# Transposing attention rows with the DMA crossbar, and a by-class layout for the dilated half

## The chip, the cores and the metric

The kernel runs on one NeuronCore of a Trainium2 chip. The metric is the device time of one execution in microseconds. The core's engines each run their own instruction stream in order: TensorE (PE; its weight loads are shown as PEld), VectorE (DVE), ScalarE (ACT), GpSimd (POOL) and SyncE (SP). SP and POOL also issue DMAs, which run on 16 DMA engines that all queues share.

## The reference

Eight heads of causal attention in eight batch rows are followed by an MLP over all tokens. Heads 0 to 3 see a sliding window of 32 positions; heads 4 to 7 see every fourth position of the last 128 (dilation 4).

```python
batch, n_heads, seq, head_dim = (8, 8, 576, 64)
rel = pos[:, None] - pos[None, :]
mask_plain = (rel >= 0) & (rel < window)                      # window = 32
mask_dil = (rel >= 0) & (rel < window * dilation) & (rel % dilation == 0)
...
attn = np.exp(scores); attn = attn / (np.sum(attn, axis=-1, keepdims=True) + 1e-09)
attn_out = np.matmul(attn, v)
x = attn_out.transpose(0, 2, 1, 3).reshape(B * S, H * D)      # 4608 x 512
h = x @ w_in                                                  # 512 x 2048
r = np.maximum(h, 0.0)
out = (r * r) @ w_out                                         # 2048 x 512
```

## The kernel before

**Two streams of work.** The program is written as a hand-interleaved order. Attention goes by batch row b, 576 tokens each. The MLP goes by chunk c of 512 tokens, nine in all. The loop at L786 takes rows 2 to 7: its iteration b runs the attention of row b, and between the attention's steps `pump(n)` issues n steps of the MLP of chunk b-1 (`moe_gen`), so that TensorE always has matmuls to do. A step is about two matmuls of 512 columns (first product, `mm1_gen`) or four of 256 columns (second product, by a Strassen-like scheme with seven block products, `mm2_strassen_gen`); a chunk has 60 steps in all, 32 of them in the first product. From row 4 on, 8 steps go ahead of the attention, 3 stand at each gap, and what is left follows at the end (`pump(1000)`). Row 3 has 16 ahead, row 2 has 24 and other gaps. Chunks 7 and 8 follow after the loop, with no attention beside them.

**A row's attention.** `attn_scores` makes the scores (`s_sliding`, L557; `s_dilated`, L576), the exponential on ACT (L547) and the mask product on DVE (L548). `attn_values` then makes the value products: three sliding ones (`av_sliding`, L605, tiles `pav`) and four dilated ones (`av_dilated`, L619, tiles `paw`), each followed by `normalize` on DVE (a reciprocal, L590, and a product, L591), which writes a tile x with tokens on partitions. All score and value tiles in PSUM come from one pool of two buffers (`papool`, tag "pa"), used in turn. Four transposing steps, `x_sliding` (L634, tiles `px`, 6 transposes each) and `x_dilated` (L652, tiles `py`, 8 each), turn x on TensorE so that features lie on partitions, and a copy on ACT (L640, L658) puts it into `xT`, a ring over four rows, in token order. `mm1_half` (L294) reads `xT` as the moving operand. As 512 is less than 576, chunk b needs most of row b as its last part.

**DVE's share of the MLP.** Each of the 16 blocks of the first product goes through a relu on ACT (L317) and a square on DVE (L318). Three larger DVE steps serve the Strassen scheme: sums of g (L327, L328), one difference in g when the second product begins (L402), and one later (L414). They stand in DVE's order where the chunk's steps put them.

**Fetching the next row.** While row b is worked on, row b+1 is fetched: `after_transposes` puts a one-element copy `seen` on POOL that waits until row b's q and k transposes have landed; behind it POOL issues the loads of the sliding q and k (`ns`, L111) and the dilated ones (`dd`, L202, into DRAM). At hook 3, after the last scores, `turn` runs: DVE regroups `ns` by token (`nr`, L119), and SP issues, in this order, its store to DRAM (`dp`, L212), the loads of v (`sv`, `sd`) and the crossbar transposes from DRAM that make `QKTp` (L220) and `QKTd` (L224), two each. All transposes stand in SP's queue.

**Stores.** A finished chunk goes out from SP, per half of 256 tokens, in rows of 2 KB (`leave`, L393); chunks 0 and 1 are stored by 128 tokens (`store`, L452). The last chunk goes out in column halves.

**Dilated classes.** The 144 positions of a class (token index modulo 4) are worked on in two blocks of 72 queries. `QD`, `PADD` and `OWND` hold these sizes.

Of the kernel before, what the change touches and what calls it, by code (L numbers as in the profile page):

```python
# [8 lines left out]
FP16 = mybir.dt.float16  # L9
# [4 lines left out]
P = 128  # L14
# [3 lines left out]
def kernel(  # L18
# [30 lines left out]
    CL = S // DIL  # L49
    QD = CL // 2  # L50
    PADD = (48, P - QD)
    OWND = (CL - 64, 64)
    KPAD = 64
# [5 lines left out]
    natp = ctx.enter_context(tc.tile_pool(name="natp", bufs=2))  # L59
    xp = ctx.enter_context(tc.tile_pool(name="xp", bufs=4))  # L60
    gp = ctx.enter_context(tc.tile_pool(name="gp", bufs=2))
# [10 lines left out]
    XW = 4 * S  # L72
    xT = const.tile([P, NDM, XW], FP16, name="xT")
    wi_cols = (512, 512, 1024)
# [58 lines left out]
    def load_dilated_v(b, eng):  # L133
        vv = v[b, HH:H].rearrange("h (i c) d -> i h (c d)", c=DIL)
        i0 = 0
        for t in range(2):
            eng.dma_start(out=sd[P - OWND[t] : P, t, :, :], in_=vv[i0 : i0 + OWND[t]])
            i0 += OWND[t]

# [115 lines left out]
    hi_ = const.tile([P, QB], FP16, name="hi_")  # L255
    md = maskd.rearrange("p (n t w) -> p n t w", t=2, w=QD)
    for m, w, pad in (
        (maskp.rearrange("p (n w) -> p n w", w=QB), QB, PADP),
        (md[:, :, 0], QD, PADD[0]),
        (md[:, :, 1], QD, PADD[1]),  # L260
    ):
        nc.vector.tensor_scalar(
            out=lo_[:, 0:w], in0=relf[:, 0:w], scalar1=-pad - 0.5, scalar2=None, op0=ALU.is_gt
        )
        nc.vector.tensor_scalar(
            out=hi_[:, 0:w], in0=relf[:, 0:w], scalar1=W - pad - 0.5, scalar2=None, op0=ALU.is_lt
        )
        nc.vector.tensor_mul(
            m,
            lo_[:, 0:w].unsqueeze(1).to_broadcast([P, m.shape[1], w]),  # L270
            hi_[:, 0:w].unsqueeze(1).to_broadcast([P, m.shape[1], w]),
        )
# [15 lines left out]
    def mm1_half(c, ffc, ph, dmks):  # L288
        lo = c * TOKC % XW
        cut = min(TOKC, XW - lo)  # L290
        parts = [(0, cut, lo)] + ([(cut, TOKC, 0)] if cut < TOKC else [])
        for dmk in dmks:
            for t0, t1, x0 in parts:
                nc.tensor.matmul(  # L294
                    ph[:, t0:t1],
                    wi4[ffc // 4][:, dmk, :, ffc % 4],
                    xT[:, dmk, x0 : x0 + t1 - t0],
                    start=(dmk == 0 and t0 == 0),
                    stop=(dmk == NDM - 1),
                    skip_group_check=len(parts) > 1,  # L300
                )
# [45 lines left out]
    w_sums = sums_of_w_out()  # L347

    def mm2_strassen_gen(c, g):
        A, Bk, Ck = "abc"  # L350
# [39 lines left out]
        def leave(o, i, js):  # L390
            t0 = c * TOKC + HTOK * i
            m = slice(HM * js[0], HM * (js[-1] + 1))
            nc.sync.dma_start(  # L393
                out=out[t0 : t0 + HTOK, m].rearrange("(t p) m -> p t m", p=P), in_=o[:, :, m]
            )

# [50 lines left out]
    def store(c, t, po):  # L447
        if t % 2 == 0:
            halves[c] = otp.tile([P, 2, DM], FP32, name=f"ot{c}_{t}", tag="ot")
        ot = halves[c][:, t % 2]  # L450
        nc.scalar.copy(ot, po)
        (nc.sync if c else nc.gpsimd).dma_start(out=out[(c * 4 + t) * P : (c * 4 + t + 1) * P, :], in_=ot)  # L452

# [113 lines left out]
    def s_dilated(b, g):  # L567
        tiles = [pa(f"pz{b}_{g}_{h}") for h in range(2)]
        for h, ps in enumerate(tiles):
            for a in range(2):  # L570
                for t in range(2):
                    q0 = KPAD + (2 * g + h) * CL + QD * t
                    for e in range(2):
                        r = slice(D * e, D * (e + 1))
                        n = 2 * a + t
                        nc.tensor.matmul(  # L576
                            ps[:, e, QD * n : QD * (n + 1)],
                            QKTd[b % 2][r, 1, a, q0 - PADD[t] : q0 - PADD[t] + P],
                            QKTd[b % 2][r, 0, a, q0 : q0 + QD],
                            start=True,  # L580
                            stop=True,
                        )
        for h, ps in enumerate(tiles):
            softmax(4 + 2 * g + h, ps, maskd)

    def normalize(b, what, pav, w):
        x = xp.tile([QB, 2, HH, D], FP16, name=f"x{b}_{what}", tag="x")
        rcp = xp.tile([QB, 2, HH], FP32, name=f"rcp{b}_{what}", tag="rcp")
        pv = pav[0:w, :, 0 : HH * (D + 2)].rearrange("p i (h d) -> p i h d", d=D + 2)
        nc.vector.reciprocal(rcp[0:w], pv[:, :, :, D])  # L590
        nc.vector.tensor_tensor(  # L591
            out=x[0:w],
            in0=pv[:, :, :, 0:D],
            in1=rcp[0:w].unsqueeze(3).to_broadcast([w, 2, HH, D]),
            op=ALU.mult,
        )
        return x

    def av_sliding(b, mp):
        pav = pa(f"pav{b}_{mp}")  # L600
        for i in range(2):
            m = 2 * mp + i
            for h in range(HH):
# [7 lines left out]
                )  # L611
        return normalize(b, f"p{mp}", pav, QB)

    def av_dilated(b, t, a):
        pav = pa(f"paw{b}_{t}_{a}")
        for e in range(2):
            for h in range(HH):
                off = e * 288 + a * 144 + t * QD
                nc.tensor.matmul(  # L619
# [5 lines left out]
                )  # L625
        return normalize(b, f"d{t}_{a}", pav, QD)

    def x_sliding(b, half, xs, wide):
        px = pt(f"px{b}_{half}", wide)
        for m3 in range(3):  # L630
            m = 3 * half + m3
            x = xs[m // 2][:, m % 2].rearrange("p h d -> p (h d)")
            for c in range(2):
                nc.tensor.transpose(  # L634
                    px[:, 288 * c + QB * m3 : 288 * c + QB * (m3 + 1)],
                    x[:, P * c : P * (c + 1)],
                    ident[0:QB, 0:QB],
                )
        t0 = (b * S + 288 * half) % XW
        nc.scalar.copy(  # L640
            xT[:, 0:2, t0 : t0 + 288],
            px[:, 0:UW].rearrange("x (c t) -> x c t", c=2),
        )

    def x_dilated(b, t, xs, wide):
        py = pt(f"py{b}_{t}", wide)
        for a in range(2):
            for e in range(2):
                x = xs[a][:, e].rearrange("p h d -> p (h d)")
                for c in range(2):  # L650
                    o = 288 * c + QD * (2 * a + e)
                    nc.tensor.transpose(  # L652
                        py[:, o : o + QD],
                        x[0:QD, P * c : P * (c + 1)],
                        ident[0:QD, 0:QD],
                    )
        t0 = (b * S + 288 * t) % XW
        nc.scalar.copy(  # L658
            xT[:, 2:4, t0 : t0 + 288].rearrange("x c (i r) -> x c i r", r=DIL),
            py[:, 0:UW].rearrange("x (c r i) -> x c i r", c=2, r=DIL),  # L660
        )
# [15 lines left out]
    def attn_values(b, gap, wide=False, hooks={}):  # L677
        xs = []
        for mp in range(3):
            xs.append(av_sliding(b, mp))  # L680
            if mp < 2:
                halo_sliding(b, mp + 1)
            else:
                halo_dilated(b, 0)
            if 4 + mp in hooks:
                hooks[4 + mp]()
            pump(gap)
        x_sliding(b, 0, xs, wide)
        halo_dilated(b, 2)
        pump(gap)  # L690
        ys = [av_dilated(b, 0, 0)]
        pump(gap)
        x_sliding(b, 1, xs, wide)
        pump(gap)
        ys.append(av_dilated(b, 0, 1))
        pump(gap)
        zs = []
        for a in range(2):
            zs.append(av_dilated(b, 1, a))
            pump(gap)  # L700
        x_dilated(b, 0, ys, wide)
        pump(gap)
        x_dilated(b, 1, zs, wide)

# [20 lines left out]
    pump(1)  # L725
    xs = [av_sliding(0, 0)]
    pump(1)
# [18 lines left out]
    for mp in (1, 2):  # L746
        xs.append(av_sliding(0, mp))
        pump(1)
    x_sliding(0, 0, xs, False)
    pump(1)  # L750
    ys = [av_dilated(0, 0, 0)]
    pump(1)
    x_sliding(0, 1, xs, False)
    pump(1)
    pending.clear()
    ys.append(av_dilated(0, 0, 1))
    zs = [av_dilated(0, 1, 0)]
    begun = [mm1_begin(0, 0)]
    zs.append(av_dilated(0, 1, 1))
    begun.append(mm1_begin(0, 1))  # L760
    x_dilated(0, 0, ys, False)
    x_dilated(0, 1, zs, False)

# [22 lines left out]
    for b in range(2, B):  # L786
# [3 lines left out]
        if nxt < B:  # L790
# [6 lines left out]
            def turn():  # L797
                dp = keep_sliding_qk(nxt, by_token(nxt, ns))
                load_v(nxt)
                transpose_sliding(nxt, dp)  # L800
                transpose_dilated(nxt, dd)
                cast_v(nxt)

            hooks[3] = turn
        first, gap, gap2 = {2: (24, 4, 2), 3: (16, 3, 3)}.get(b, (8, 3, 3))
        pump(first)
        attn_scores(b, gap, 0, hooks)
        attn_values(b, gap2, False, hooks)
        pump(1000)
# [33 lines left out]
```

The softmax here doesn't subtract the row's maximum and nothing guards it: scores larger than these inputs give would overflow.

## Time and profile before

| what | us |
|---|---|
| median of three runs | 309.6 (309.18 to 309.9) |
| the profiled execution | 309.11 |
| its span in the trace | 307.3 |
| PE busy | 290.7 |
| DVE busy | 207.9 |
| ACT busy | 183.4 |
| POOL busy | 71.7 |
| L294, 512 columns, mean of one of 512 | 0.380 (pipelined: 64 follow each other in 13.81) |
| L591, product of a normalization, mean | 0.687 |
| L640 and L658, copies of transposed x, mean | 0.64 |
| QKTp transposes, issue to landing, median of 12 | 6.5 |
| QKTd transposes, issue to landing, median of 12 | 3.9 |

The span is what the trace covers; 1.8 us of the execution lie around it. [...]consecutive matmuls start closer together than their durations say. The first matmuls of the chunks 2 to 7 mark the iterations: 94.55, 126.29, 157.48, 188.75, 219.94 and 251.13 us. DMA engines are busy for nine tenths or more in most slices up to about 225 us, and little after that. SP's queue shows issues only; a long one means that the issue itself or what it waits for takes that time.

### The profile page before, as it was taken

What the parts mean: (1) busy time and instruction counts of PE and PEld (TensorE: products, weight loads), DVE (VectorE), ACT (ScalarE), POOL (GpSimd) and SP (SyncE); (2) the same over time, 40 slices, a digit from 0 to 9 for tenths busy, and PEclk for the clock granted to TensorE, in tenths of its full rate; (3) what the DMA queues carried; (4) which work ended last, traced back from release to release, by engine and by line L of the source; (5) the groups of instructions that cost most, each with busy time, mean ns of one, the idle gap of its engine ahead of it and who ended that gap; (6) DMA issues with size and microseconds to landing.
All of it is one profiled execution on the core that took longest, in us unless ns stands there. A gap on an engine that the chain in (4) does not pass through costs nothing.

```text
span 307.3 us, 7108 instructions
## 1 busy us (share of the span) xinstructions
PE 290.7 (95%) x2874; PEld 196.5 (64%) x2874; DVE 207.9 (68%) x433; ACT 183.4 (60%) x326; POOL 71.7 (23%) x114
## 2 busy tenths in 40 slices
PE   1798998999999999999999999999999999999994
PEld 1454554554455469656998997569756975785583
DVE  7784448568953798489748983898378934834652
ACT  2766648668645982598339834983499336425620
POOL 4481008413805303400630083007000000000000
PEclk9999999999999999999999999999999999999999
DMA  7899997999699999999968996889500020003004
GB/s 116 188 200 213 206 171 114 189 241 205 112 214 194 222 199 185 240 154 191 171 130 188 181 184 97 219 166 186 165 10 2 0 109 29 0 4 136 2 0 137
DMA packets 67024, 43.58 MB, mean 142 GB/s; under 512 B 48624, under 2 KB 59376, under 8 KB 66992
## 3 DMA queue, kind: packets, MB, share of 16 engines
q1 hardware_dynamic: 57920, 28.45, 44.9%
q0 software_dynamic: 9072, 14.68, 27.7%
q8 instruction: 22, 0.36, 0.5%
q14 instruction: 10, 0.08, 0.1%
HBM read 36.70 MB, written 16.52 MB: 173 GB/s over the span
## 4 chain that ended last, share of the span: by engine, by line
PE 71%; ACT 10%; DVE 7%; DMA 6%; issue 2%; SPq 2%; POOL 1%; POOLq 0%; DVEq 0%
PE ph L294 27%; PE pa L371 16%; PE pb L371 8%; PE po L437 7%; ACT AT L547 5%; DMA ns<-in_q_dram 5%; PE pc L371 4%; ACT rt L317 3%; PE paw L619 3%; PE pav L605 2%; PE px L634 1%; PE py L652 1%; DVE AT L548 1%; DMA QKTp<-dp 1%; PE pf L491 1%
## 5 line engine op out<-in xcount | busy, mean ns | idle before, releaser
L294 PE MATMUL ph<-xT,wi 128*128 128x512 f16 (+1 forms) x640 | 133.4, 359 | 0.7 <-ACT xT L658 0.7
L317 ACT ACTIVATE rt<-ph 128x512 f16<-128x512 f32 x144 | 84.9, 603 | 33.5 <-PE ph L294 33.5
L294 PEld LDWEIGHTS <-wi 128*128 128x128 f16 x640 | 68.6, 114 | 46.8 <-issue 0.8
L318 DVE TENSOR_TENSOR g<-rt 128x512 f16<-128x512 f16 x144 | 62.2, 435 | 42.7 <-ACT rt L317 41.1
L371 PEld LDWEIGHTS <-g 128*128 128x128 f16 x448 | 42.5, 98 | 5.3
L170 POOL CAST vp<-sv 128x512 f16<-128x512 f32 x24 | 17.5, 760 | 108.6 <-DMA sv<-in_v_dram 62.1
L371 PEld LDWEIGHTS <-gs 128*128 128x128 f16 x336 | 31.6, 98 | 3.7 <-DVE gs L328 0.3
L437 PE MATMUL po<-wo,g 128*128 128x512 f16 x128 | 33.1, 379 | 0.0
L398 DVE TENSOR_TENSOR ov<-pb,ov 128x512 f32<-128x512 f32 x14 | 9.7, 691 | 29.9 <-PE pb L371 18.2
L371 PE MATMUL pa<-wt,gs 128*128 128x256 f16 x224 | 28.5, 273 | 0.0
L371 PE MATMUL pb<-wt,g 128*128 128x256 f16 x224 | 27.7, 273 | 0.0
L178 POOL CAST vd<-sd 128x512 f16<-128x512 f32 (+1 forms) x32 | 24.2, 782 | 3.1 <-DMA sd<-in_v_dram 2.4
L387 ACT COPY ov<-pa 128x512 f32<-128x512 f32 x14 | 8.2, 585 | 26.8 <-PE pa L371 26.8
L591 DVE TENSOR_TENSOR x_d<-paw,rcp_d 72x512 f16<-72x512 f32 x32 | 22.0, 687 | 1.1
L547 ACT ACTIVATE AT<-pz 128x576 f16<-128x576 f32 x32 | 20.0, 712 | 1.7 <-PE pz L576 1.6
L548 DVE TENSOR_TENSOR AT<-AT,maskp 128x576 f16<-128x576 f16 x32 | 17.3, 545 | 5.1 <-ACT AT L547 2.6
L547 ACT ACTIVATE AT<-ps 128x576 f16<-128x576 f32 x32 | 19.2, 662 | 1.2 <-PE ps L557 0.9
L658 ACT COPY xT<-py 128x576 f16<-128x576 f16 x16 | 10.2, 640 | 14.7 <-PE py L652 14.6
L591 DVE TENSOR_TENSOR x_p<-pav,rcp_p 96x512 f16<-96x512 f32 x24 | 16.5, 687 | 0.8
L387 ACT COPY ou<-pa 128x512 f32<-128x512 f32 x14 | 8.2, 588 | 14.5 <-PE pa L371 14.5
L548 DVE TENSOR_TENSOR AT<-AT,maskd 128x576 f16<-128x576 f16 x32 | 14.9, 484 | 2.6 <-ACT AT L547 0.6
L640 ACT COPY xT<-px 128x576 f16<-128x576 f16 x16 | 10.2, 638 | 9.2 <-PE px L634 8.6
(81 smaller groups left out, 306.6 us busy)
## 6 DMA issues: line engine op xcount, KB each, us to landing
sv<-in_v_dram SPq DMA_DIRECT2D x14, 288.0 KB, 6.2
dp<-nr SPq DMA_DIRECT2D x12, 288.0 KB, 4.1
out_dram<-ou SPq DMA_DIRECT2D x6, 512.0 KB, 3.1
out_dram<-ov SPq DMA_DIRECT2D x6, 512.0 KB, 3.5
sd<-in_v_dram SPq DMA_DIRECT2D x8, 320.0 KB, 7.3
ns<-in_k_dram POOLq DMA_DIRECT2D x8, 288.0 KB, 5.2
ns<-in_q_dram POOLq DMA_DIRECT2D x8, 288.0 KB, 6.4
sd<-in_v_dram SPq DMA_DIRECT2D x8, 256.0 KB, 6.7
```

Source lines behind the costliest of these rows:

```text
L170: nc.gpsimd.tensor_copy(vp[b % 2][:, m : m + 2, :, 0:D], sv[:, :, m : m + 2, :].rearrange("p h m d -> p m h d"))
L178: nc.gpsimd.tensor_copy(vd[b % 2][p0:P, t, c : c + 2, :, 0:D], sd[p0:P, t, :, D * c : D * (c + 2)].rearrange("p h (c d) -> p c h d", d=D),)
L294: nc.tensor.matmul(ph[:, t0:t1], wi4[ffc // 4][:, dmk, :, ffc % 4], xT[:, dmk, x0 : x0 + t1 - t0], start=(dmk == 0 and t0 == 0), stop=(dmk ...
L317: nc.scalar.activation(rt, ph[:], ACTF.Relu)
L318: nc.vector.tensor_mul(g[:, ffc, :], rt, rt)
L371: nc.tensor.matmul(banks[bank][:, t], a(k, t), b(k), start=(new and t == 0 and k == 0), stop=(k == HF - 1), skip_group_check=True,)
L387: nc.scalar.copy(ot, banks[A])
L437: nc.tensor.matmul(po, g[:, ffc, t * P : (t + 1) * P], wo[ffc // 4][:, ffc % 4, :], start=(ffc == 0), stop=(ffc == NFF - 1),)
L547: nc.scalar.activation(AT[:, u, 0:UW], ps[:, :, 0 : UW // 2], ACTF.Exp, scale=scale)
L548: nc.vector.tensor_mul(AT[:, u, 0:UW], AT[:, u, 0:UW], mask)
L591: nc.vector.tensor_tensor(out=x[0:w], in0=pv[:, :, :, 0:D], in1=rcp[0:w].unsqueeze(3).to_broadcast([w, 2, HH, D]), op=ALU.mult,)
L640: nc.scalar.copy(xT[:, 0:2, t0 : t0 + 288], px[:, 0:UW].rearrange("x (c t) -> x c t", c=2),)
```

## The change

From row 3 on, x isn't transposed on TensorE any more. `attn_values_by_dma` collects the three sliding results in one tile and the dilated ones in two, and SP issues four crossbar transposes from SBUF to SBUF: two for the sliding half after the third value product, and one after each pair of dilated ones. They stand in SP's queue among those of the next row's q and k: xTp twice, QKTp twice (`turned`), xTd, xTd, QKTd twice (`done`). Rows 0 to 2 keep TensorE's transposes.

The dilated half of x is kept by class (`xTd`: class, feature block, position), the sliding half in token order (`xTp`). `mm1_half` lets a chunk's columns go class by class: for the sliding half it reads every fourth column of `xTp` in four runs, for the dilated half it reads runs of `xTd`. A row of the first product's output, and so of the final one, is then a token of class r at position i; the four classes of a position are neighbouring tokens, and the store writes two classes of a position as one 4-KB run (`rows_of`). Chunks 0 and 1 are stored by two such pieces each, instead of four. The last chunk keeps column halves. The dilated blocks become 80 and 64 queries wide instead of 72 and 72.

```diff
-    QD = CL // 2
-    PADD = (48, P - QD)
-    OWND = (CL - 64, 64)
+    QD = (80, 64)
+    Q0D = (0, 80)
+    PADD = (48, 64)
...
-    xp = ctx.enter_context(tc.tile_pool(name="xp", bufs=4))
+    xp = ctx.enter_context(tc.tile_pool(name="xp", bufs=2))
...
-    xT = const.tile([P, NDM, XW], FP16, name="xT")
+    xTp = const.tile([P, 2, XW], FP16, name="xTp")
+    xTd = const.tile([P, DIL, 2, XW // DIL], FP16, name="xTd")
...
     def mm1_half(c, ffc, ph, dmks):
-        lo = c * TOKC % XW
-        cut = min(TOKC, XW - lo)
-        parts = [(0, cut, lo)] + ([(cut, TOKC, 0)] if cut < TOKC else [])
+        lo = c * TOKC % XW // DIL
+        ni = TOKC // DIL
+        cut = min(ni, XW // DIL - lo)
+        parts = [(0, cut, lo)] + ([(cut, ni, 0)] if cut < ni else [])
+        pr = ph.rearrange("x (r i) -> x r i", r=DIL)
         for dmk in dmks:
-            for t0, t1, x0 in parts:
+            for i0, i1, x0 in parts:
+                x1 = x0 + i1 - i0
+                if dmk < 2:
+                    x = xTp[:, dmk, DIL * x0 : DIL * x1].rearrange("x (i r) -> x r i", r=DIL)
+                else:
+                    x = xTd[:, :, dmk - 2, x0:x1]
                 nc.tensor.matmul(
-                    ph[:, t0:t1],
+                    pr[:, :, i0:i1],
                     wi4[ffc // 4][:, dmk, :, ffc % 4],
-                    xT[:, dmk, x0 : x0 + t1 - t0],
+                    x,
...
+    def rows_of(c):
+        return out[c * TOKC : (c + 1) * TOKC, :].rearrange("(i r) m -> i r m", r=DIL)
...
-            nc.sync.dma_start(
-                out=out[t0 : t0 + HTOK, m].rearrange("(t p) m -> p t m", p=P), in_=o[:, :, m]
-            )
+            nc.sync.dma_start(out=rows_of(c)[:, 2 * i : 2 * i + 2, m], in_=o[:, :, m])
...
-        (nc.sync if c else nc.gpsimd).dma_start(out=out[(c * 4 + t) * P : (c * 4 + t + 1) * P, :], in_=ot)
+        if t % 2:
+            (nc.sync if c else nc.gpsimd).dma_start(out=rows_of(c)[:, t - 1 : t + 1], in_=halves[c])
...
+    def x_tiles(b):
+        x = xp.tile([QB, 2, NB, 2, D], FP16, name=f"xs{b}", tag="xs")
+        return x, [xp.tile([QD[t], DIL, HH, D], FP16, name=f"xd{b}_{t}", tag=f"xd{t}") for t in range(2)]
...
+    def x_sliding_by_dma(b, xs):
+        t0 = b * S % XW
+        for c in range(2):
+            nc.sync.dma_start_transpose(
+                out=xTp[:, c, t0 : t0 + S].rearrange("x (m q) -> x m q", q=QB),
+                in_=xs[0][:, c].rearrange("p m e d -> p (m e d)"),
+            )
+
+    def x_dilated_by_dma(b, t, xs):
+        i0 = b * CL % (XW // DIL) + Q0D[t]
+        nc.sync.dma_start_transpose(
+            out=xTd[:, :, :, i0 : i0 + QD[t]].rearrange("x r c i -> x (r c) i"),
+            in_=xs[1][t].rearrange("p r h d -> p (r h d)"),
         )
...
+    def attn_values_by_dma(b, gap, then=(None, None)):
+        xs = x_tiles(b)
+        for mp in range(3):
+            av_sliding(b, mp, xs)
+            if mp < 2:
+                halo_sliding(b, mp + 1)
+            else:
+                for c in (0, 2):
+                    halo_dilated(b, c)
+            pump(gap)
+        x_sliding_by_dma(b, xs)
+        if then[0]:
+            then[0]()
+        for t in range(2):
+            for a in range(2):
+                av_dilated(b, t, a, xs)
+                pump(gap)
+            x_dilated_by_dma(b, t, xs)
+        if then[1]:
+            then[1]()
...
             def turn():
-                dp = keep_sliding_qk(nxt, by_token(nxt, ns))
+                kept.append(keep_sliding_qk(nxt, by_token(nxt, ns)))
                 load_v(nxt)
-                transpose_sliding(nxt, dp)
+
+            def turned():
+                transpose_sliding(nxt, kept[0])
+
+            def done():
                 transpose_dilated(nxt, dd)
                 cast_v(nxt)
...
-        attn_values(b, gap2, False, hooks)
+        if b == 2:
+            turned()
+            done()
+            attn_values(b, gap2)
+        else:
+            attn_values_by_dma(b, gap2, (turned, done) if nxt < B else (None, None))
```

## The prediction

> **What bounds the kernel now.** I read the page's busy shares and chain of waits first, then the windows cut at the starts of rows 3 to 7's iterations, then the timelines of TensorE, VectorE and SyncE in one such iteration. "Row" is a batch row b; its iteration runs the attention of row b among the matmuls of chunk b-1.
>
> ```profile
> PE 290.7 (95%) x2874; PEld 196.5 (64%) x2874; DVE 207.9 (68%) x433; ACT 183.4 (60%) x326; POOL 71.7 (23%) x114
> PE 71%; ACT 10%; DVE 7%; DMA 6%; issue 2%; SPq 2%; POOL 1%; POOLq 0%; DVEq 0%
> ```
>
> ```profile
> 94.55:126.29 31.74, 31.37 (x317) 21.78 (x316) 23.66 (x47) 21.00 (x38) 10.20 (x18) 1.00 1.10 197
> 126.29:157.48 31.19, 31.04 (x318) 21.94 (x317) 23.32 (x48) 19.99 (x37) 9.42 (x16) 1.00 0.98 176
> 188.75:219.94 31.19, 31.04 (x318) 21.88 (x316) 23.32 (x48) 19.99 (x37) 6.58 (x8) 1.00 0.85 169
> 219.94:251.13 31.19, 31.04 (x317) 21.90 (x316) 22.82 (x47) 19.99 (x37) 0.00 (x0) 1.00 0.10 35
> ```
>
> The columns are length, then busy time of PE, PEld, DVE, ACT, POOL, clock, DMA share, GB/s. TensorE fills every iteration (31.04 of 31.19), so removed matmuls should shorten it, if nothing else stands right behind TensorE. VectorE's 23.3 looks roomy, but that is a mean. In row 6's values part it is not:
>
> ```profile
> 202.64 0.42 PE L605 MATMUL pav<-vp,AT 128*128 128x65 f16 x8
> ...
> 205.75 0.41 PE L619 MATMUL paw<-vd,AT 128*128 128x65 f16 x8
> ...
> 212.01 0.42 PE L619 MATMUL paw<-vd,AT 128*128 128x65 f16 x8
> ...
> 213.57 0.42 PE L652 MATMUL py<-ident,x_d 72*128 72x72 f16 x8
> 213.83 1.48 PE L371 MATMUL pa<-wt,gs 128*128 128x256 f16 x12
> ```
>
> ```profile
> 199.56 0.75 DVE L119 COPY nr<-ns 128x2304 f16<-128x2304 f16 x1
> ...
> 205.27 0.69 DVE L591 TENSOR_TENSOR x_p<-pav,rcp_p 96x512 f16<-96x512 f32 x1
> ...
> 209.44 1.21 DVE L402 TENSOR_TENSOR g<-g 128x2048 f16<-128x2048 f16 x1
> ...
> 210.80 0.69 DVE L591 TENSOR_TENSOR x_d<-paw,rcp_d 72x512 f16<-72x512 f32 x1
> ...
> 212.70 0.69 DVE L591 TENSOR_TENSOR x_d<-paw,rcp_d 72x512 f16<-72x512 f32 x1
> ```
>
> From 198.6 to 213.4 VectorE has no gap between instructions (14.07 busy of 14.80 in that window). The last value product starts at 212.01 and the PSUM buffer it needs (two "pa" buffers in turn) was freed at 211.49, by the second dilated normalization: 0.5 us of room. So VectorE is a second bound just behind TensorE there.
>
> The third thing to see is the loop that fetches the next row, here for row 4 (SyncE, then GpSimd):
>
> ```profile
> 110.65 1.16 SPq L212 DMA_DIRECT2D dp<-nr  x2
> ...
> 116.34 5.70 SPq L220 DMA_TRANSPOSE QKTp<-dp  x2
> 122.13 3.75 SPq L224 DMA_TRANSPOSE QKTd<-dd  x2
> ```
>
> ```profile
> 128.26 0.19 POOL L231 COPY seen<-QKTd 128x1 f16<-128x1 f16 x1 [4.02 <-DMA QKTd<-dd]
> ...
> 129.47 0.62 POOL L111 DMA_DIRECT2D ns<-in_q_dram  x1
> ```
>
> SyncE issues without a pause from dp to QKTd; then `seen` on GpSimd waits for QKTd to land, and behind it in GpSimd's order stand the loads of the row after. `seen` came at 101.68, 128.26 and 155.28 in rows 3, 4, 5: the loop turns in about 26.6 to 27 us, against 31.2 for an iteration.
>
> **What the Trainium skill says.** *SBUF — State Buffer*, "Door 1: The DMA port swizzle": SBUF is read in 16-byte lines, at full rate if at least two accesses fall in each. The new moving operand steps 8 bytes (4 fp16), so just two. The trace has no strided moving operand; its nearest is the weight of the same line, also at a step of 8 bytes: 114 ns a load, against 98 for packed ones. *DMA: Bandwidth & Descriptors*, "Latency and other measured facts": a DMA transpose moved 261 GB/s in one kernel. While transposes ran here, windows of 2 us showed 174 to 203 GB/s, all traffic together. The same page, "Issuing engines are not separate DMA queues": every queue shares the same 16 engines, so the new transposes compete with the V loads; the share of 1.1 to 1.3 from 204 to 214 agrees. *TensorE: Matmul & The Clock Gate*, "Back-to-back issue gap": 512 columns take about 216 ns start to start; 64 matmuls in 13.81 us agree.
>
> **The change, part by part.**
>
> *TensorE.* Rows 3 to 7 lose two px batches (6 transposes) and two py batches (8). A py batch moves its follower from 213.57 to 213.83; px the same: 0.26 us each. That is 4 x 0.26 = 1.04 us per row, 5.2 in all. ACT loses four copies of 0.64 per row, from stretches where it already waits for TensorE: nothing.
>
> *Where the values now stand.* Without the px steps the seven value products stand only three steps of chunk work apart (a step is 4 matmuls of 256 columns or 2 of 512, 0.4365 us). The last stands at step 38 instead of 44, so six steps go from ahead of it to behind it. VectorE's order up to the second dilated normalization keeps all its work but L402 (1.21), which falls behind. VectorE has no gap there, so that normalization ends at 211.49 - 1.21 = 210.28. TensorE would like to start the last value product at about 209.0 and has to wait until 210.3 for the buffer. After it come 0.25 us of its own and 60 - 38 = 22 steps, 9.60: the next chunk starts at 220.15. Before: 212.01 + 0.25 + 16 steps (6.98) + 0.52 of py = 219.76. So the 1.04 us is eaten and 0.4 lost, in each of rows 4 to 7: +1.6. In row 3 the fifth value product waits instead (its buffer comes free at 117.05, where TensorE would be at 115.4): 117.1 + 0.25 + 1.31 + 0.25 + 1.31 = 120.2 for the last one, + 0.25 + 14 steps (6.1) = 126.57, against 126.13: +0.4.
>
> *Four transposes more on SyncE* in rows 3 to 6, amid this loop (row 7 has nothing behind them). No SBUF source is in the trace. They move 590 KB, as much as the QKTd pair, whose issue took 2.7 to 3.75 us (mean 3.1); I take X = 3.5, as there are four. Bounds: 590 KB at 261 GB/s, 2.3; and the QKTp pair under load, 6.
>
> *First use.* Chunk b needs both xTp transposes of row b and, as 80 of the 144 positions suffice, the first xTd, not the second. In row 3 QKTp's issue ended at 122.04; with two xTp (1.75) and xTd (0.95) it is 124.7, and 2.2 to land (QKTd of row 5: issue ended 183.66, `seen` 185.89), plus up to 0.7 as xTp waits for the normalization at 117.05: 127.0 to 127.6. Needed at 126.57 + 0.43 = 127.0: 0.3 taken. In rows 4 to 6 the same count gives 2 us of room.
>
> *The loop.* Row 4's `seen` moves from 128.26 to 131.8. The load's second half is issued 1.2 later and takes 6.7: 139.7. In VectorE's order nr stands 10.97 after the chunk's first matmul (199.56 - 188.59), so at about 137.7 here, with 0.5 us hidden behind a wait for ACT (row 7, without nr, shows 0.46 idle there). VectorE then waits 1.5, and everything behind it (g, the normalizations) too; with VectorE the bound, TensorE pays it in full: +1.5. After that the loop, 26.6 + 3.5 = 30.1, is shorter than the iteration of 31.6 and catches up: nothing in rows 5 and 6.
>
> *Cheap parts.* The strided moving operand (288 matmuls): nothing, as two accesses per line; bounds 0 and 15 ns each (4.3), the gap of the weight loads. Stores in 4-KB runs: the store is off the path except the last, whose runs stay 1 KB: nothing. 80/64 instead of 72/72: same columns and elements per partition: nothing. The one xs tile in rows 0 to 2 may make px wait for a later normalization, 0 to 0.3.
>
> *Sum:* 1.6 + 0.4 + 0.3 + 1.5 = +3.8 us on the profiled 309.1 (span 307.3 and 1.8 around it): 312.9. The median of the runs is 0.5 above that execution: 313.4.
>
> **Rivals.** (1) *TensorE's saving is paid out* (faster). The two PSUM buffers don't bind because VectorE gets ahead (ACT's copies are gone, g comes earlier), and X is near 2.3 so nr isn't late. For it: 31.04 of 31.19 busy; against: the gapless VectorE stretch. Gives 309.6 - 5.2 = 304.4, with half of it 307. (2) *The crossbar loop becomes the bound.* With X = 6, row 3's first use stalls 1.8, nr in row 4 comes 2.5 late, and the loop of 32.6 costs 1 us more in each of two rows: 2.0 + 1.8 + 2.5 + 2 = 8.3, so 318. It decides from X = 5 on, where 26.6 + X passes 31.6. For it: DMA share above 1 exactly where the four go; against: QKTd's short issues. (3) *The strided read costs.* At 15 ns in 288 matmuls, 4.3 more than the forecast: 317.7; it adds up fully, since TensorE is full in those stretches. For it: 114 against 98 ns; against: the two accesses per line.
>
> **How the numbers follow.** The forecast (VectorE's wait and a late nr; 310.5 to 315.5) 0.52, rival 1 0.24, rival 2 0.14, rival 3 0.10. 0.2% is about what can be told from no change here. Faster takes rival 1's better part, 0.22; same takes 0.05 from its edge and the forecast's; slower the rest, 0.73. The range of eight in ten cuts half of rival 1 and the worst of 2 and 3: 306.5 to 319. The forecast's own range is 310.5 to 315.5.
>
> **What would show it.** Right: in rows 4 to 7 the last dilated value product waits about 1.2 us for a VectorE normalization; the px and py batches are gone but the iterations take 31.4 to 31.7 us; nr in row 4 idles VectorE for its load; the first dilated transposes land before the chunk that needs them. Wrong: value products without a wait and iterations near 30.1; issues of the new transposes near 1.5 us each or more; or starts of 512-column matmuls on xTp more than 216 ns apart.

## The result and the profile after

| what | us |
|---|---|
| after, median of 4 runs | 374.66 (373.94 to 375.4) |
| before, median of 4 runs beside them | 309.75 |
| ratio, with its 95% interval | 1.207 (1.199 to 1.216) |
| span of the profiled execution after | 372.2 (before: 307.3) |

The change made the kernel 65 us slower. The forecast was 313.4 with a range up to 319, so the sign was right and the size was not. Four of the runs reported here (one each of before and a_spaced, two of f2_half) lay over 1.5% above the fastest of their kernel, and the ratios leave them out. The page of after, first the busy shares, then the shares of the chain of waits:

```profile
PE 354.0 (95%) x2734; PEld 193.1 (52%) x2734; DVE 210.2 (56%) x433; ACT 176.1 (47%) x306; POOL 72.6 (19%) x112
PE 87%; DVE 8%; ACT 2%; DMA 1%; issue 1%; POOL 0%; SPq 0%; POOLq 0%
```

TensorE runs 140 matmuls fewer and is busy 63 us longer, while every other engine keeps about its busy time. Nearly all of the time is inside TensorE's own instructions; little of it is waiting, and none is the clock:

```profile
109.00:147.16 38.16, 37.51 (x290) 20.87 (x288) 22.85 (x47) 19.27 (x34) 8.13 (x12) 1.00 0.80 150
147.16:185.64 38.48, 37.50 (x289) 20.89 (x288) 24.24 (x48) 18.58 (x33) 9.69 (x14) 1.00 0.91 171
224.50:263.00 38.50, 37.50 (x290) 20.86 (x288) 24.26 (x48) 18.57 (x33) 8.35 (x11) 1.00 0.82 151
263.00:300.89 37.89, 37.50 (x289) 20.87 (x288) 23.10 (x47) 18.57 (x33) 0.00 (x0) 1.00 0.21 45
```

These are the iterations of rows 3, 4, 6 and 7, with the columns of the windows shown before the result. Each has 27 or 28 matmuls fewer than before and still 6.1 us (row 3) to 6.5 us (the others) more of busy TensorE, at a clock of 1.00. Rows 4 to 7 also hold 0.4 to 1.1 us in which TensorE is idle, against 0.1 or 0.2 before. The groups kept apart by shape say which matmuls:

```profile
L300 PE MATMUL ph<-xTp,wi 128*128 128x512 f16 x256 | 136.7, 624 | 0.0
L300 PE MATMUL ph<-xTd,wi 128*128 128x512 f16 x256 | 78.3, 387 | 0.9 <-ACT xTd L662 0.9
```

Same line, same shape, same type, same weights; only the moving operand differs. On xTd, read in packed runs, one takes 387 ns, as before the change (380). On xTp, read at every fourth column, it takes 624 ns. These durations overlap (before, 64 matmuls of 0.380 us follow each other in 13.81 us), so the cost is read better from starts. TensorE's timeline in chunk 7, where no attention stands beside the matmuls (start, length, and the count of matmuls merged in a line):

```profile
300.73 1.07 PE L300 MATMUL ph<-xTp,wi 128*128 128x512 f16 x2
301.62 0.61 PE L300 MATMUL ph<-xTd,wi 128*128 128x512 f16 x2
302.07 1.07 PE L300 MATMUL ph<-xTp,wi 128*128 128x512 f16 x2
302.96 0.61 PE L300 MATMUL ph<-xTd,wi 128*128 128x512 f16 x2
```

Two on xTp hold the array for 301.62 - 300.73 = 0.89 us, two on xTd for 302.07 - 301.62 = 0.45: 0.45 us against 0.22 for one. The chain of waits gives the sum over the 64 matmuls of a first product, for chunks 7 and 8, before and after:

```profile
251.13 13.81 PE ph L294 x64
...
277.17 13.81 PE ph L294 x64
```

```profile
300.89 21.43 PE ph L300 x64
...
334.55 21.46 PE ph L300 x64
```

That is 7.62 us more in chunk 7 (7.65 in chunk 8), 0.238 us for each of the 32 strided matmuls. All 9 x 32 = 288 make 68.6 us, if they cost as much beside attention as here. The measured difference is 64.9, so about -3.7 is left to explain. The experiments separate the stride from the rest.

### The profile page after: what moved, and what is told of

Read it like the earlier page. It is cut to its first block, busy times and chain, and to the rows that moved or that the text cites. A ratio compares the mean times of both kernels' runs of the same rounds, so it can differ in the third digit from the quotient of the medians.

```text
span 372.2 us, 6857 instructions
## 1 busy us (share of the span) xinstructions
PE 354.0 (95%) x2734; PEld 193.1 (52%) x2734; DVE 210.2 (56%) x433; ACT 176.1 (47%) x306; POOL 72.6 (19%) x112
## 4 chain that ended last, share of the span: by engine, by line
PE 87%; DVE 8%; ACT 2%; DMA 1%; issue 1%; POOL 0%; SPq 0%; POOLq 0%
PE ph L300 53%; PE pa L380 11%; PE po L443 7%; PE pb L380 7%; PE pc L380 2%; PE paw L629 2%; PE ps L564 1%; PE pz L583 1%; PE pav L613 1%; DVE AT L555 1%; DVE gs L333 1%; DVE gs L334 1%; DMA sv<-in_v_dram 1%; ACT rt L323 1%; DVE xd L601 1%; DVE xs L601 1%
## 5 line engine op out<-in xcount | busy, mean ns | idle before, releaser
L300 PE MATMUL ph<-xTp,wi 128*128 128x512 f16 (+1 forms) x320 | 154.0, 580 | 0.0
L300 PEld LDWEIGHTS <-wi 128*128 128x128 f16 x640 | 70.0, 115 | 104.6 <-issue 73.8
L300 PE MATMUL ph<-xTd,wi 128*128 128x512 f16 (+1 forms) x320 | 88.2, 365 | 0.9 <-ACT xTd L662 0.9
L380 PEld LDWEIGHTS <-gs 128*128 128x128 f16 x336 | 32.5, 98 | 3.7
L380 PE MATMUL pa<-wt,gs 128*128 128x256 f16 x224 | 26.9, 272 | 0.0
L177 POOL CAST vd<-sd 128x512 f16<-128x512 f32 (+1 forms) x32 | 25.8, 832 | 2.9 <-DMA sd<-in_v_dram 2.4
L601 DVE TENSOR_TENSOR xd<-paw,rcp_d 80x512 f16<-80x512 f32 (+1 forms) x32 | 21.9, 684 | 1.1
L554 ACT ACTIVATE AT<-pz 128x576 f16<-128x576 f32 x32 | 19.1, 650 | 4.4 <-PE pz L583 4.3
L629 PEld LDWEIGHTS <-AT 128*128 128x128 f16 x256 | 11.8, 98 | 12.4 <-issue 6.4
L629 PE MATMUL paw<-vd,AT 128*128 128x65 f16 x256 | 13.2, 193 | 4.2 <-DVE xd L601 3.5
```

The source lines that it names most:

```text
L177: nc.gpsimd.tensor_copy(vd[b % 2][p0:P, t, c : c + 2, :, 0:D], sd[p0:P, t, :, D * c : D * (c + 2)].rearrange("p h (c d) -> p c h d", d=D),)
L300: nc.tensor.matmul(pr[:, :, i0:i1], wi4[ffc // 4][:, dmk, :, ffc % 4], x, start=(dmk == 0 and i0 == 0), stop=(dmk == NDM - 1), skip_group_ ...
L380: nc.tensor.matmul(banks[bank][:, t], a(k, t), b(k), start=(new and t == 0 and k == 0), stop=(k == HF - 1), skip_group_check=True,)
L554: nc.scalar.activation(AT[:, u, 0:UW], ps[:, :, 0 : UW // 2], ACTF.Exp, scale=scale)
L601: nc.vector.tensor_tensor(out=x, in0=pv, in1=rb, op=ALU.mult)
L629: nc.tensor.matmul(pav[:, e, h * (D + 2) : h * (D + 2) + D + 1], AT[:, 4 + h, off : off + P], vd[b % 2][:, t, 2 * a + e, h, 0 : D + 1], st ...
```

## The experiments

Two theories stood at the start. **Theory S**: the strided read of the moving operand alone makes the 65 us, and the rest of the change costs what the forecast said. **Rival R**: part of the 65 us comes from the layout and the order (the writing of the first product by class, the crossbar transposes, the value products' order, the stores), and a packed read would leave much of it. A third question was what about the step costs the time, and whether a place for the reordering exists that is free.

### The change without the stride, the stride without the change

`a_packed` is the kernel after with one run of packed columns in place of four runs at a step of four:

```diff
-                    x = xTp[:, dmk, DIL * x0 : DIL * x1].rearrange("x (i r) -> x r i", r=DIL)
+                    x = xTp[:, dmk, DIL * x0 : DIL * x1].rearrange("x (r i) -> x r i", r=DIL)
```

> The changed kernel with one thing undone: the moving operand of the sliding half is read packed (step 1) instead of every fourth column, in the same four runs. This mixes tokens of the two halves in a column, so the outputs differ; the count and size of all instructions stay. Theory 'step' (a moving step of 8 bytes doubles a matmul of 512 columns; the last two chunks show 21.43 us for 64 matmuls against 13.81, 0.238 us for each of the 288 strided ones): 374.7 - 68.6 = 306 us, and xTp matmuls at the same spacing as xTd ones. Rival 'crossbar' (the new transposes and the fetching loop set the end): still above 350. My forecast without its third rival: 313.4.

`b_strided` is the kernel before, with the step put into the reads of the sliding half and nothing else:

```diff
-                    xT[:, dmk, x0 : x0 + t1 - t0],
+                    xT[:, dmk, x0 : x0 + t1 - t0].rearrange("x (i r) -> x r i", r=DIL)
+                    if dmk < 2
+                    else xT[:, dmk, x0 : x0 + t1 - t0],
```

> The kernel before with one thing added: the sliding half of xT is read at a step of 4 elements in the first product, no DMA and no layout changed. It mixes tokens of the two halves in a column. Theory 'step': 309.6 + 68.6 = 378 us. Rival 'crossbar': 309.6 as before. Were the new layout's four PSUM runs to blame, it would be 309.6 too.

| kernel | us | against before |
|---|---|---|
| a_packed, 4 runs | 314.58 (313.54 to 315.33) | 1.014 (1.009 to 1.019) of 309.6 |
| b_strided, 1 run | 374.84 | 309.6 beside it |
| after, 4 runs | 374.66 | 1.207 (1.199 to 1.216) of 309.75 |

The stride alone gives the whole result. Without it 60 us are gone and about 5 remain (2.6 to 5.8 by the interval), where the forecast without the stride had 3.8. Both sums of the expectations miss, though: 306 for a_packed was 8.6 too low, and 378 for b_strided 3.2 too high. The groups of a_packed by shape no longer tell the two operands apart:

```profile
L300 PE MATMUL ph<-xTp,wi 128*128 128x512 f16 x256 | 76.4, 380 | 0.0
L300 PE MATMUL ph<-xTd,wi 128*128 128x512 f16 x256 | 76.2, 380 | 0.7 <-ACT xTd L662 0.7
```

and the first product of chunk 8 in the chain of b_strided has the length that it has in after:

```profile
335.27 21.44 PE ph L294 x64
```

So the -3.7 of the sum above isn't a gain of the rest: the stride alone came out 3.4 below its 68.6. Most of that lies in the iterations of rows 3 to 7. In b_strided they take 192.47 us, where the 156.58 of before and 5 x 7.62 make 194.7. Of these 2.2 us, 0.9 are short idle times of TensorE that before had and b_strided has filled. What the remainder comes from isn't shown.

The 5 us of a_packed and the 65 us of b_strided add up to 70, not 65. The windows say why. Over the same five iterations TensorE in b_strided is busy for all but 0.04 of the 192.47 us, in after for 187.8 of 191.9. The lower busy time, 0.9 us a row, is the saving of the dropped transposes. Waits of value products for VectorE, 0.4 to 1.1 us long and 4.2 in all, give most of it back. Saving and waits are both there in after, 0.6 us apart. What a_packed pays beyond that is mostly a load that comes late in row 4 (below); in after, where an iteration is about 7 us longer, that load keeps nothing waiting.

### What about the step costs the time

`s_steps` is the kernel before, except that in chunks 7 and 8 each group of four blocks reads x at another step:

```diff
+        step = {7: (1, 2, 3, 4), 8: (1, 4, 6, 8)}.get(c, (1, 1, 1, 1))[ffc // 4]
...
+                    x = xT[:, dmk, 0 : n * step].rearrange("x (i r) -> x r i", r=step)[:, 0 : 512 // n]
```

> The kernel before; only in chunks 7 and 8, which have no attention beside them, groups of four blocks of the first product read xT at steps of 1, 2, 3, 4 (chunk 7) and 1, 4, 6, 8 elements (chunk 8), from other columns, so the outputs of these chunks differ. Sixteen matmuls per group. If two accesses per 16-byte line were enough, steps 2, 3 and 4 take 3.45 us a group like step 1, and 6 and 8 more. If a line serves only four accesses at full rate: 2 free, 3 at 1.5 times, 4 at twice, 6 at 3 times, 8 at four times (or twice, if the rate stops falling at one 16-byte line per access, or at 8 bytes). If any step but 1 costs the double: 2 and 3 like 4, 7.3 us a group.

The relu of a block starts when its four matmuls are done, so the starts on ACT pace them. From ACT's timeline of s_steps, pairs at steps 2, 3, 4 and 8 columns (start, length, and in brackets the wait before):

```profile
259.96 0.60 ACT L322 ACTIVATE rt<-ph 128x512 f16<-128x512 f32 x1 [0.31 <-PE ph L299]
260.88 0.60 ACT L322 ACTIVATE rt<-ph 128x512 f16<-128x512 f32 x1 [0.32 <-PE ph L299]
...
264.52 0.60 ACT L322 ACTIVATE rt<-ph 128x512 f16<-128x512 f32 x1 [0.77 <-PE ph L299]
265.88 0.60 ACT L322 ACTIVATE rt<-ph 128x512 f16<-128x512 f32 x1 [0.76 <-PE ph L299]
...
270.87 0.60 ACT L322 ACTIVATE rt<-ph 128x512 f16<-128x512 f32 x1 [1.22 <-PE ph L299]
272.69 0.60 ACT L322 ACTIVATE rt<-ph 128x512 f16<-128x512 f32 x1 [1.22 <-PE ph L299]
...
315.53 0.60 ACT L322 ACTIVATE rt<-ph 128x512 f16<-128x512 f32 x1 [3.02 <-PE ph L299]
319.15 0.60 ACT L322 ACTIVATE rt<-ph 128x512 f16<-128x512 f32 x1 [3.02 <-PE ph L299]
```

A quarter of such a distance, averaged over a group, is one matmul. At a step of two it is 0.226 us, hardly more than packed; from there the cost grows with the step. `s_lines` asks whether it is the step or the 16-byte lines (8 columns of fp16) that are touched. It takes long steps in chunk 7, and in chunk 8 columns that lie in groups: two of every four, four of every eight, two of every eight.

```diff
+        kind = {7: ("1", "12", "16", "32"), 8: ("1", "2of4", "4of8", "2of8")}.get(c, ("",) * 4)[ffc // 4]
```

> As s_steps, in chunks 7 and 8 alone, outputs of these chunks differ: steps of 1, 12, 16 and 32 elements (chunk 7), and packed, 2 of every 4, 4 of every 8 and 2 of every 8 elements (chunk 8), 16 matmuls of 512 columns per group. s_steps gave 0.216, 0.226, 0.341, 0.454, 0.679 and 0.903 us a matmul at steps 1, 2, 3, 4, 6, 8. If the reader passes over every byte of the span, 4.5 bytes in the time of a column: 12, 16 and 32 take 1.36, 1.81 and 3.6 us. If it fetches lines of 16 bytes: all three stay near 0.90; with lines of 32 bytes they stop at 1.81. 2 of 4 and 4 of 8 span as much as a step of 2: 0.226; 2 of 8 as a step of 4: 0.454.

ACT's timeline of s_lines, pairs at a step of 12, at a step of 32, and at two of every eight:

```profile
263.94 0.60 ACT L326 ACTIVATE rt<-ph 128x512 f16<-128x512 f32 x1 [2.98 <-PE ph L303]
267.52 0.60 ACT L326 ACTIVATE rt<-ph 128x512 f16<-128x512 f32 x1 [2.98 <-PE ph L303]
...
289.25 0.60 ACT L326 ACTIVATE rt<-ph 128x512 f16<-128x512 f32 x1 [2.84 <-PE ph L303]
292.69 0.60 ACT L326 ACTIVATE rt<-ph 128x512 f16<-128x512 f32 x1 [2.84 <-PE ph L303]
...
328.53 0.60 ACT L326 ACTIVATE rt<-ph 128x512 f16<-128x512 f32 x1 [1.22 <-PE ph L303]
330.34 0.60 ACT L326 ACTIVATE rt<-ph 128x512 f16<-128x512 f32 x1 [1.22 <-PE ph L303]
```

The two kernels took 342.35 and 350.27 us (1 run each); what counts is the cost of one matmul of 512 fp16 columns in them. The third column counts the 16-byte lines in the order of reading: steps of six and more take the 512 columns in two to eight runs over one stretch, and a line that a later run comes back to counts again.

| columns read | us | lines | ns a line |
|---|---|---|---|
| packed | 0.216 | 64 | 3.4 |
| every 2nd | 0.226 | 128 | 1.77 |
| 2 of 4 | 0.227 | 128 | 1.77 |
| 4 of 8 | 0.229 | 128 | 1.79 |
| every 3rd | 0.341 | 192 | 1.78 |
| every 4th | 0.454 | 256 | 1.77 |
| 2 of 8 | 0.454 | 256 | 1.77 |
| every 6th | 0.679 | 384 | 1.77 |
| every 8th | 0.903 | 512 | 1.76 |
| every 12th | 0.895 | 512 | 1.75 |
| every 16th | 0.92 | 512 | 1.80 |
| every 32nd | 0.86 | 512 | 1.68 |

One rule fits all rows: a matmul takes the longer of 0.42 ns a column and about 1.77 ns a line (1.68 to 1.80). The size of the line comes out of the table: the cost stops growing at a step of eight columns, which is 16 bytes. Four fp16 columns in a line are enough for nearly the full rate, two halve it, one quarters it, and beyond one column per line a longer step costs no more. Two of eight costs what every fourth does, so it is the lines that count and not the distance between neighbours. In after, each of the four runs takes two columns from every line: the same 64 lines as a packed read, but each comes up four times, 256 in all, and 0.454 - 0.216 = 0.238 is the price. Nearly all matmuls at steps of 8 to 32 ran at a granted clock of 0.50 (last section); the step of six, which ran at both clocks, took the same time at each.

### Is the reordering free at the other end?

The classes must be interleaved with the token order somewhere. `f1_psum` reads both halves of x packed and lets the sliding half's product write by class into PSUM, its columns 512 bytes apart:

```diff
-                    x = xTp[:, dmk, DIL * x0 : DIL * x1].rearrange("x (i r) -> x r i", r=DIL)
+                    x = xTp[:, dmk, DIL * x0 : DIL * x1].rearrange("x (i r) -> x i r", r=DIL)
...
-                    pr[:, :, i0:i1],
+                    pr[:, :, i0:i1].rearrange("x r i -> x i r") if dmk < 2 else pr[:, :, i0:i1],
```

> The changed kernel with the reordering moved from the read to the write: the sliding half is read packed in token order and its product is written to PSUM at the place of its class (4 columns 512 bytes apart, then the next position). The result is the reference's. If a strided PSUM write is free: 306 us as with the packed read. If it costs as the strided read does: 375. More if every write of a 4-byte value to another line costs more than that.

`f5_psum16` keeps the columns in token order and lets the dilated half's product write every fourth column, 16 bytes apart (its stores are in 2-KB runs again):

```diff
+                    po = ph[:, DIL * i0 : DIL * i1]
...
+                    po = ph[:, DIL * i0 : DIL * i1].rearrange("x (i r) -> x r i", r=DIL)
```

> The changed kernel with a packed read of both halves, columns in token order, and the dilated half's product written to PSUM every fourth column (16 bytes apart) instead; stores of 2-KB rows as before. The result is the reference's. f1_psum wrote 512 bytes apart and took 369. If the cost is one of PSUM lines of a few bytes, 16 bytes apart costs as much: about 369. If it grows with the step, it is much less: 315 to 330.

They took 368.96 and 368.84 us (1 run each, against 309.6 and 310.19 before). The first product of chunk 8 in the chains of f1_psum and of f5_psum16:

```profile
330.39 20.64 PE ph L300 x64
```

```profile
330.19 20.64 PE ph L302 x64
```

Both pay (20.64 - 13.81) / 32 = 0.213 us more for each strided write. With the packed 0.216 that is 0.84 ns a column, twice the packed time, and a step 32 times as long costs the same. A write out of order is about as dear as a read out of order here, and neither is a free place.

### What the rest of the change costs

In a_packed the iterations of rows 4 to 6 are these:

```profile
128.95:162.99 34.04, 30.54 (x290) 20.71 (x289) 23.12 (x48) 17.92 (x33) 9.40 (x12) 1.00 1.01 189
162.99:194.53 31.54, 30.44 (x353) 27.45 (x352) 23.05 (x48) 17.88 (x33) 9.26 (x12) 1.00 0.98 182
194.53:226.03 31.50, 30.32 (x290) 20.72 (x288) 23.05 (x48) 17.86 (x33) 9.19 (x12) 1.00 0.99 186
```

TensorE is busy 0.5 to 0.7 us less than before, and yet rows 5 and 6 take 31.5 us, as the forecast had them (31.6), with the waits in the place it named; row 4 takes 34.04. TensorE's timeline of a_packed in row 5, an earlier value product and the last one:

```profile
180.38 0.41 PE L629 MATMUL paw<-vd,AT 128*128 128x65 f16 x8 [0.16 <-DVE xs L601]
...
184.51 0.41 PE L629 MATMUL paw<-vd,AT 128*128 128x65 f16 x8 [0.84 <-DVE xd L601]
```

That a wait stands there doesn't show that the order makes it. `a_spaced` is a_packed with the value products as far apart as before: the gaps of the two px steps, which stood between value products, are given back. Like a_packed it mixes tokens, so it serves to measure and not to be used.

```diff
+        pump(gap)
...
-                pump(gap)
+                pump(gap if t or a else 2 * gap)
```

> The packed read (as a_packed, same mixing of tokens), and two gaps of chunk work put back where the px steps stood, so that the value products stand as many steps apart as before the change. Theory 'VectorE's order' (the last value product waits for a PSUM buffer because the steps between the products went with the px steps): no value product waits, rows 5 to 7 take 30.2 to 30.5 us instead of 31.5, row 4 still pays some 2 us for its late nr; 307 to 309 in all. Rival (the extra time of a_packed is crossbar traffic alone): as a_packed, 314.6.

It took 309.73 us (median of 20 runs; before 310.19 in 36 runs; ratio 0.996, 0.993 to 0.999). Its iterations of rows 4 to 6, the first one cut at the chunk's second pair of matmuls:

```profile
129.23:161.45 32.22, 30.23 (x288) 20.45 (x288) 22.43 (x47) 17.92 (x33) 9.02 (x12) 1.00 1.07 192
161.45:191.68 30.23, 30.12 (x353) 27.57 (x352) 23.08 (x48) 17.76 (x33) 9.04 (x12) 1.00 1.05 192
191.68:221.82 30.14, 29.99 (x289) 20.89 (x288) 23.05 (x48) 17.75 (x33) 9.15 (x12) 1.00 1.02 190
```

Rows 5 to 7 fall to 30.1 or 30.2, 1.0 below before, and in them no value product waits for a normalization. So the whole TensorE saving was there, and the order of the value products against VectorE's queue had eaten it. Row 4 doesn't fall with them: counted from its first matmul, at 127.70, it takes 33.75 us. Its first dilated product waits for the crossbar, in TensorE's timeline of a_spaced:

```profile
129.23 0.59 PE L300 MATMUL ph<-xTd,wi 128*128 128x512 f16 x2 [1.11 <-DMA xTd<-xd]
```

and in VectorE's timeline nr waits for its load as the forecast had it, for 2.40 us; this is the line from a_packed:

```profile
142.30 0.76 DVE L120 COPY nr<-ns 128x2304 f16<-128x2304 f16 x1 [2.40 <-DMA ns<-in_q_dram]
```

Behind nr in VectorE's order stand a square, for which a relu on ACT waits, and the first normalization of row 4, which frees a PSUM buffer. In a_packed the relu and the normalization are both done at 144.57, and the third sliding value product, after 1.64 us of waiting, starts at 144.71; the trace names the relu as what it waited for. The wait for xTd is seen in a_spaced alone: in a_packed the first matmul on xTd starts 0.51 us after the two before it, only 0.08 later than usual, as row 3 itself takes longer there (32.32 us against 30.97). So in a_packed the 2.5 us that row 4 takes beyond rows 5 and 6 go with the late nr.

`a_from4` tests whether row 3's transposes on SP make row 4 late: it is a_spaced with row 3's x transposed on TensorE.

```diff
-        if b == 2:
+        if b <= 3:
```

> As a_spaced (packed read that mixes tokens, value products as far apart as before), but row 3's x is transposed on TensorE as in rows 0 to 2; the crossbar takes rows 4 to 7. a_spaced has rows 5 to 7 at 30.1 to 30.2 us and row 4 at 33.8. Theory 'late nr' (the four transposes of row 3 delay `seen` of row 4, so its nr waits 2.4 us for its load, and xTd of row 3 comes 1.1 late): row 4 falls to 30.2 to 30.6, row 3 is 31.7 as before the change, 306 in all. Rival (the first row by crossbar costs this, whichever it is, or row 4 is slow for another reason): the 33.8 stays in row 4 or moves to row 5, and the time stays near 309.

It took 306.88 us (306.47 to 309.44, 4 runs; before 311.13 in 7 runs; ratio 0.989, 0.983 to 0.995). GpSimd's `seen` for row 4 in a_spaced and in a_from4, and the window of row 4's iteration in a_from4:

```profile
134.82 0.31 POOL L230 COPY seen<-QKTd 128x1 f16<-128x1 f16 x1 [9.10 <-DMA QKTd<-dd]
```

```profile
129.09 0.19 POOL L230 COPY seen<-QKTd 128x1 f16<-128x1 f16 x1 [4.05 <-DMA QKTd<-dd]
```

```profile
127.63:157.77 30.14, 29.99 (x291) 20.94 (x289) 23.04 (x48) 17.74 (x33) 8.82 (x12) 1.00 1.03 183
```

`seen` comes 5.7 us earlier. Row 4 is now as short as rows 5 to 7 (30.14 to 30.36), and its nr does not wait. One row by crossbar too early had cost row 4 in the way that the forecast named: row 3's transposes stand before QKTd in SP's queue, and GpSimd's loads of the next row stand behind `seen`.

### A version that beats both

Of the change's parts, the crossbar transposes pay if the value products stay spaced, and the class order of the columns paid in none of the three ways tried (a strided read, and two strided writes). `f2_half` is the kernel before with the sliding half alone transposed by the crossbar, from row 4 on and straight into xT's token order, with px's gaps kept and SP's order QKTp, xT, QKTd. The dilated half stays on TensorE, so every read and write is packed.

```diff
+    def x_sliding_by_dma(b, xs):
+        t0 = b * S % XW
+        for c in range(2):
+            nc.sync.dma_start_transpose(
+                out=xT[:, c, t0 : t0 + S].rearrange("x (m q) -> x m q", q=QB),
+                in_=xs[:, c].rearrange("p m e d -> p (m e d)"),
+            )
...
-        x_sliding(b, 0, xs, wide)
+        if by_dma:
+            x_sliding_by_dma(b, xd)
+            if then:
+                then()
+        else:
+            x_sliding(b, 0, xs, wide)
```

> The kernel before with part of the change alone: in rows 4 to 7 the sliding half of x is transposed by the crossbar into token order (packed read), the px matmuls and copies go, their gaps stay; issue order on SP is QKTp, xTp, QKTd. The dilated half stays on TensorE, store and layout stay. The result is the reference's. Expected from 2 x 0.26 us of TensorE per row in four rows: 309.6 - 2.1 = 307.5, if xTp lands before the next chunk starts and nr isn't late. If the crossbar loop costs: 310 or more.

It took 308.35 us (median of 15 runs; before 310.19; ratio 0.993, 0.990 to 0.996), against an expected 307.5. Each iteration from row 4 on loses the two px batches of 0.26, and nothing takes their place (the chain of f2_half, first matmuls of chunks 3 to 7):

```profile
127.10 3.47 PE ph L294 x16
...
157.77 3.51 PE ph L294 x32
...
188.53 3.47 PE ph L294 x16
...
219.19 3.47 PE ph L294 x16
...
249.87 13.81 PE ph L294 x64
```

These iterations take 30.67, 30.76, 30.66 and 30.68 us, against 31.19 before (31.27 in row 5).

## Why the prediction was right or wrong

**The step that failed** is the first of the "cheap parts": "The strided moving operand (288 matmuls): nothing, as two accesses per line; bounds 0 and 15 ns each (4.3)". It was 238 ns each, 16 times the upper bound. The lower bound came from the Trainium skill, *SBUF — State Buffer*, "Door 1: The DMA port swizzle", which asks for at least two accesses per 16-byte line. The lines are indeed what counts, but for TensorE's moving operand two fp16 accesses per line give half the rate, and four are needed (0.454, 0.226 and 0.216 us at a step of four, of two and packed). The measurement decides against the page here. The upper bound was the second fault: it was taken from strided weight loads, 114 against 98 ns in the same trace. The difference is 16 (the prediction has 15), and it is for 128 columns, loaded beside running matmuls. Scaled to 512 columns, which is an estimate, it would give 64 ns, still about a quarter of what was measured: another reader is no bound for this one. The third rival had the right place and mechanism ("it adds up fully, since TensorE is full in those stretches"), with that bound as its size. It had 10 in a hundred. The sign of being wrong that the prediction gave for it, starts of 512-column matmuls on xTp more than 216 ns apart, is what the timeline shows: 0.45 us.

**The other terms** could be read once the stride was out of the way; a_packed at 314.6 is the kernel as the forecast saw it, with a free read, and 313.4 was forecast for that. In the profiled executions its rows 3 to 7 take 0.6, 2.85, 0.3, 0.3 and 0.3 us more than before, 4.3 in all; the forecast had 0.7, 1.9, 0.4, 0.4 and 0.4, or 3.8. So the terms were about right, and not only their sum; row 4 alone was sized too small.

- *TensorE's saving of 1.04 a row*: there. The iterations of a_spaced are 30.14 to 30.23, 1.0 below before.
- *The value products wait for VectorE, about 1.2 us, iterations of 31.6*: 0.84 + 0.16 us in a_packed at the products named, iterations of 31.5; gone when the products are spaced.
- *X, the four transposes on SP, 3.5 us*: from the store dp to `seen` it took 21.6 and 21.0 us in rows 4 and 5 of a_packed, against 17.6 and 17.4 before, so 4.0 and 3.6.
- *nr in row 4 late by 1.5*: late by 2.4, and row 4 took 2.5 more than rows 5 and 6 in a_packed; the order and the loop that make it late hold (a_from4).
- *First use of xTd, 0.3*: 0.08 in a_packed. It was 1.11 in a_spaced, where row 3 had no other waits to cover it.
- *The loop catches up after that*: yes, rows 5 and 6 show no wait for a load.
- *Stores, 80 and 64 columns, one xs tile*: the 5 us of a_packed leave no room for them that can be told. About 2 us of its profiled span lie before chunk 2 begins (96.63 against 94.55). s_steps and s_lines, whose program up to chunk 7 is that of before, also start chunk 2 at 97.05 and 96.43, so an execution's own scatter is as large as this, and nothing there can be put down to the change.

Left open: what scatters in the first 95 us; why the strided matmuls beside attention cost a little less than those in chunks 7 and 8; and whether a layout with four or more neighbouring tokens of a class in each line could keep the whole change's saving, which was not tried.

## What to carry to other kernels

Count the 16-byte lines that a moving operand touches, in the order of reading, before its columns: a step inside a matmul that is already the bound costs nearly in full, and moving the step to the output costs nearly the same. When an access pattern isn't in the trace, bound it with the reader that will do it; another reader at the same step is no bound, and when the part stands on the full engine a wide bound must go into the range. And when steps are taken off the first engine, keep the distance between products that wait for the second: with the packed read, the same kernel was 1.4% slower or 0.4% faster than before by the gaps alone.

## What the hardware showed beyond that

- The read of the moving operand has one price for all steps: 1.77 ns per 16-byte line against 0.42 ns per column, so a matmul at a step of eight or more takes four times as long. Strided writes into PSUM cost 0.84 ns per column at 16 and at 512 bytes alike.
- At steps of six and more the granted clock fell to 0.50, although the trace shows TensorE busy without a pause; at steps of three and four it stayed at 1.00 over the few us of their groups. What makes it fall isn't shown. Two windows of s_steps, at steps of four and then six, and of six alone (length, busy PE, PEld, DVE, ACT, POOL, clock, DMA share, GB/s):

```profile
296.00:302.00 6.00, 6.00 (x12) 1.07 (x10) 1.28 (x3) 1.43 (x3) 0.00 (x0) 0.97 0.00 0
302.00:308.00 6.00, 6.00 (x10) 1.11 (x9) 0.85 (x2) 1.19 (x2) 0.00 (x0) 0.50 0.01 3
```

The strided matmuls of s_steps don't feel it: those at a step of six are 0.679 us apart on both sides of 302. The packed ones behind them do, until the clock is back. In the chain of s_steps the first 16 matmuls of the second product take 3.21 us, where others take 1.75:

```profile
322.72 3.21 PE pa L376 x16
325.93 0.87 PE pc L376 x8
326.80 1.75 PE pa L376 x16
```

In after, where strided and packed matmuls alternate by twos, the clock stayed at 1.00.
